# Sliding-window attention on one core: one reciprocal for each query block in place of one for two blocks with lane shuffles

## The chip, the cores and the metric

The kernel runs on one core of one Trainium2 chip. The metric is the device time of one execution in microseconds. The kernel before took 613.11 us in the median of three runs (611.52 to 613.53).

In what follows, TensorE (PE) does the matmuls, VectorE (DVE), ScalarE (ACT) and GpSimd (POOL) the rest of the arithmetic, and SyncE (SP) issues most DMAs. PEld stands for TensorE's weight loads. [...]

## What is computed

Two independent attention problems, A and B, each with its own x, wqkv and wo, in bf16. The outputs stand side by side in the last axis. With S = 2048, D = 1024, 32 heads of 32 columns and a window of 256 keys:

```python
def _A_ref(x, wqkv, wo):
    B, S, D = x.shape
    H = 32; Dh = D // H; W = 256
    qkv = (x @ wqkv).reshape(B, S, 3, H, Dh).transpose(2, 0, 3, 1, 4)
    q, k, v = qkv[0], qkv[1], qkv[2]
    scores = jnp.einsum("bhqd,bhkd->bhqk", q, k) * (Dh ** -0.5)
    idx = jnp.arange(S)
    mask = (idx[:, None] - idx[None, :] >= 0) & (idx[:, None] - idx[None, :] < W)
    scores = jnp.where(mask[None, None], scores, -1e9)
    p = _softmax(scores, axis=-1)
    o = jnp.einsum("bhqk,bhkd->bhqd", p, v)
    return o.transpose(0, 2, 1, 3).reshape(B, S, D) @ wo
```

## The kernel before

**Tiles.** The sequence is cut into 16 blocks of 128. With a window of 256, the queries of block q see the keys of blocks q, q - 1 and q - 2: the first under the diagonal mask, the second whole, the third under the opposite mask. A key block j therefore meets query blocks j, j + 1 and j + 2, and such a pair (j, q) is called an entry. Four heads of 32 columns make a head group g of 128 columns; there are 8 groups in each problem, 16 in all, with 45 entries each.

**Sessions.** Entries are taken in a fixed order, four at a time (SLOTS). One such step is a session, and there are 180. `session` (L438) makes on TensorE the scores of four heads for its four entries into the one tile `st` (L451), ScalarE makes the exponential of all of it into a tile `pt` (L459), and GpSimd sets the masked triangles of the diagonal and of the far entries to zero (L467, L471). GpSimd also does a one-element memset ahead of each DMA that a session starts (L350), which orders the load behind the tile's former users.

**Values and row sums.** `pv` (L486) handles a pair of query blocks p (2p and 2p + 1; 8 pairs in each group, 128 calls) three sessions after the pair's last entry. It takes a bank `acc` (two buffers, so each call needs the one that the call before last used) and accumulates in it, with one 32-column weight tile for each of the four heads, the products of `pt` with V in columns 0 to 255. The row sums of the softmax are matmuls too, with weights of ones. To spare some of them, `edge` (L477) has VectorE add the diagonal entry and the far entry of each query block into the tile `both` (L481) a session earlier, so that a block needs one sum over `both` and one over the middle entry. The call with p = 0 of each group has no far entries and takes no `both`; its sums come straight from `pt`.

The two query blocks of a pair share one area of 128 columns for their row sums: the weights `ones` are two tiles of 32 columns, one with ones in columns 0 to 15 and zeros in the others, one the other way round. So of the 32 lanes of a head, lanes 0 to 15 hold the sums of the first block and lanes 16 to 31 those of the second. VectorE makes one reciprocal of that area into `rinv` (L524). Two lane shuffles (L529) then spread lane 0 or lane 16 over all 32 lanes of a head and so make `wide`, 256 columns. One multiplication (L531) turns `acc` and `wide` into the normalised `oT`, which ends the use of the bank.

**What else TensorE does.** The projections run in chains of eight matmuls or more (L170, in one piece at L172 or in four column pieces at L176): Q and K of a head group, V of two groups, and the output. A chain fills a bank `pp` (two buffers), which ScalarE (L190) or VectorE (L192) then empties with a cast to bf16. After a Q or K chain VectorE also ORs the result's bits into `top` (L184), from which a certificate is made that the fixed shift in the exponential is safe.

**What sets the order.** The kernel is unrolled, and each engine runs its instructions in the order in which the program writes them. For each session the loop at L600 writes: chains that are due (`forced`, L418), the session, the `pv` calls that are due (ahead of which `finish_norm(1)` writes what is left of all but the latest normalisation), the edges due in the next session, and then matmuls of chains up to a budget from `level` (L426). Budgets count the constants NS_MM, NS_ROW and NS_PV and the sizes of the chains.

The planner keeps a model of the time on each engine (`_Clock`, L60). Two things are chosen by it. Which engine empties a bank is the one that would be done first:

```python
best = min(engines, key=lambda e: max(getattr(self, e), self.pe) + COST[e])
```

And small pieces of VectorE's work wait in the list `side` (the ORs, and for each `pv` call the pieces of its normalisation, which go ahead of the ORs). `emit` writes one of them after a matmul step whenever VectorE's modelled time is less than 100 ns ahead of TensorE's or more than eight pieces wait. COST (L37) holds the modelled price of each piece in ns: "rinv" for a reciprocal, "mult" for the shuffles and the multiplication together.

Of the kernel before, what the change touches and what calls it, by code (L numbers as in the profile page):

```python
# [8 lines left out]
BF16 = mybir.dt.bfloat16  # L9
F32 = mybir.dt.float32  # L10
# [3 lines left out]
ALU = mybir.AluOpType  # L14
# [4 lines left out]
P = 128  # L19
# [7 lines left out]
QB = 4  # L27
# [6 lines left out]
PV_LAG = 3  # L34
FREE = 10 ** 6
ACT_EXP = 1800.0
COST = {"act": 590.0, "dve": 670.0, "or": 560.0, "rinv": 930.0, "mult": 900.0,  # L37
        "edge": 620.0}


# [19 lines left out]
class _Clock:  # L60
# [10 lines left out]
    def evacuate(self, engines):  # L71
        best = min(engines, key=lambda e: max(getattr(self, e), self.pe) + COST[e])
        end = max(getattr(self, best), self.pe + 150.0) + COST[best]
        setattr(self, best, end)
# [4 lines left out]
def _fast_path(ctx, tc, cfg, problems, outs, consts, certify):  # L79
    nc = tc.nc  # L80
# [6 lines left out]
    ones = consts["ones"]  # L87
# [23 lines left out]
    vp = ctx.enter_context(tc.tile_pool(name="vt", bufs=2 * NQ))  # L111
    ptp = ctx.enter_context(tc.tile_pool(name="pt", bufs=7))
    edgep = ctx.enter_context(tc.tile_pool(name="edge", bufs=2))
    normp = ctx.enter_context(tc.tile_pool(name="norm", bufs=1))
    osbp = ctx.enter_context(tc.tile_pool(name="osb", bufs=4))
    once = ctx.enter_context(tc.tile_pool(name="once", bufs=1))
    ps_st = ctx.enter_context(tc.tile_pool(name="ps_st", bufs=1, space=PSUM))
    ps_acc = ctx.enter_context(tc.tile_pool(name="ps_acc", bufs=2, space=PSUM))
    ps_proj = ctx.enter_context(tc.tile_pool(name="ps_proj", bufs=2, space=PSUM))

    xT, wqk, wv, wo_sb, vts, oTs, qks, pts = {}, {}, {}, {}, {}, {}, {}, {}
    edges = {}
# [204 lines left out]
    pieces = {}  # L327
# [34 lines left out]
    for m in range(NM):  # L362
        for b in range(0, NB, 512 // (VG * P)):
            k = b // QB
# [5 lines left out]
    for pi in range(NPROB):  # L370
        final = pi == NPROB - 1
        for b in range(NB):
            k = b // QB
# [112 lines left out]
    def pv(g, p):  # L486
        pi, t = divmod(g, T)
        m, u = divmod(g, VG)
        k, h = divmod(p, QB // 2)
        segs = []  # L490
        for j in range(max(2 * p - 2, 0), 2 * p + 2):
            for q in range(max(j, 2 * p), min(j + 3, 2 * p + 2)):
                s, a = place(g, j, q)
                if segs and segs[-1][0] == j and segs[-1][2] == s:
                    segs[-1][4] += 1
                else:
                    segs.append([j, q, s, a, 1])
        acc = ps_acc.tile([P, 512], F32, name="acc")
        clock.pe = max(clock.pe, clock.norms.pop(0))
        moves = [(None, j, (q - 2 * p) * P, n * P, pts[s][:, :, a:a + n, :])  # L500
                 for (j, q, s, a, n) in segs]
        for (j, q, s, a, n) in segs:
            for i in range(n):
                if p == 0 or q + i == j + 1:
                    moves.append((q + i - 2 * p, j, 2 * P, P, pts[s][:, :, a + i:a + i + 1, :]))
        if p:
            both = edges.pop((g, p))
            moves += [(h, 0, 2 * P, P, both[:, :, h:h + 1, :]) for h in range(2)]
        for x, (h, j, o, w_, src) in enumerate(moves):
            for r in range(4):  # L510
                c = u * P + 32 * r
                lhsT = vts[(m, j // QB)][:, j % QB, c:c + 32] if h is None else ones[:, h, :]
                nc.tensor.matmul(acc[32 * r:32 * r + 32, o:o + w_], lhsT=lhsT,  # L513
                                 rhs=src[:, r, :, :], start=(x == 0), stop=(x == len(moves) - 1),
                                 tile_position=(0, 32 * r), skip_group_check=True)
            clock.pe += NS_PV * w_ / P
        if (pi, k) not in oTs:
            oTs[(pi, k)] = opool.tile([P, T, 512], BF16, name="oT")
        rinv = normp.tile([P, P], F32, name="rinv")
        wide = normp.tile([P, 256], F32, name="wide")  # L520
        pieces = []

        def f():
            nc.vector.reciprocal(out=rinv[:], in_=acc[:, 2 * P:3 * P])  # L524
        pieces.append((COST["rinv"], f, False))

        def f():
            for h in range(2):
                nc.vector.stream_shuffle(out=wide[:, h * P:(h + 1) * P], in_=rinv[:],  # L529
                                         mask=[16 * h] * 32)  # L530
            nc.vector.tensor_tensor(out=oTs[(pi, k)][:, t, (p % 2) * 256:(p % 2 + 1) * 256],  # L531
                                    in0=acc[:, 0:256], in1=wide[:], op=ALU.mult)
        pieces.append((COST["mult"], f, True))
        n = max([i + 1 for i, x in enumerate(side) if x[2]], default=0)
        side[n:n] = pieces
# [28 lines left out]
    warm = ps_proj.tile([P, 512], F32, name="pp")  # L564
    for _ in range(5):
        nc.tensor.matmul(warm[:], lhsT=blank[:, 0:P], rhs=blank[:, 0:512], start=True, stop=True)
    flips = [ps_acc.tile([P, 512], F32, name="acc") for _ in range(2)]
    flips = [f[:] for f in flips]
    flips.append(ps_st.tile([P, 4, SLOTS, P], F32, name="st")[:, 0].rearrange("p a q -> p (a q)"))
    flips.append(None)  # L570
    held = [{}, {}]

    def flip(a):
        if a == 3:
            flips[a] = ps_acc.tile([P, 512], F32, name="acc")[:]
        f = flips[a].bitcast(BF16).rearrange("p (ct q) -> p ct q", q=P)
        for ct in range(CT):
            nc.tensor.transpose(out=f[:, ct, :], in_=xrow[a][:, ct * P:(ct + 1) * P],  # L578
                                identity=ident[:])
        dst = xT[(0, 0)][:, :, a * P:(a + 1) * P]  # L580
        half = CT // 2
        nc.scalar.copy(out=dst[:, :half, :], in_=f[:, :half, :])
        nc.vector.tensor_copy(out=dst[:, half:, :], in_=f[:, half:, :])
# [16 lines left out]
    for now in range(END):  # L600
# [3 lines left out]
        while due and due[0][0] <= now:  # L604
            _, pg, pk = due.pop(0)
# [14 lines left out]
    while due:  # L620
        _, pg, pk = due.pop(0)
# [131 lines left out]
@with_exitstack  # L753
def kernel(
    ctx: ExitStack,
    tc: tile.TileContext,
    A_x: bass.AP,
    A_wqkv: bass.AP,
    A_wo: bass.AP,
    B_x: bass.AP,  # L760
    B_wqkv: bass.AP,
    B_wo: bass.AP,
    out: bass.AP,
):
    nc = tc.nc
    S, D = A_x.shape[-2], A_x.shape[-1]
    cfg = _Cfg(S, D)
    problems = [(x.flatten_outer_dims(), wqkv, wo)
                for (x, wqkv, wo) in ((A_x, A_wqkv, A_wo), (B_x, B_wqkv, B_wo))]
    of = out.flatten_outer_dims()  # L770
    outs = [of[:, pi * D:(pi + 1) * D] for pi in range(len(problems))]

    cpool = ctx.enter_context(tc.tile_pool(name="consts", bufs=1))
    ones = cpool.tile([P, 2, 32], BF16, name="ones")
    nc.vector.memset(ones[:], 0.0)
    nc.vector.memset(ones[:, 0, 0:16], 1.0)
    nc.vector.memset(ones[:, 1, 16:32], 1.0)
    ones1 = cpool.tile([P, 1], F32, name="ones1")
    nc.vector.memset(ones1[:], 1.0)
    pm = cpool.tile([P, 1], F32, name="pm")  # L780
    okp = cpool.tile([P, 1], F32, name="okp")
    unsafe_i = cpool.tile([1, 1], I32, name="unsafe_i")
    ident = cpool.tile([P, P], BF16, name="ident")
    nc.gpsimd.memset(ident[:], 0.0)
    nc.gpsimd.affine_select(out=ident[:], in_=ident[:], pattern=[[-1, P]],
                            compare_op=ALU.not_equal, fill=1.0, base=0, channel_multiplier=1)
    consts = {"ones": ones, "ident": ident}
    assert DH * QK_LIMIT * QK_LIMIT * cfg.scale <= CERT

    def reduce_bits(top):  # L790
        seen = top[:]
        nc.vector.tensor_single_scalar(out=seen, in_=seen, scalar=0x7FFF7FFF, op=ALU.bitwise_and)
        nc.vector.tensor_reduce(out=pm[:], in_=seen.bitcast(I16), axis=AX.X, op=ALU.max)
        nc.vector.tensor_scalar(out=okp[:], in0=pm[:], scalar1=float(QK_LIMIT_BITS), scalar2=None,
                                op0=ALU.is_lt)

    def decide(pool):
        csum = pool.tile([P, 512], F32, name="pp")
        nc.tensor.matmul(csum[0:1, 0:1], lhsT=ones1[:], rhs=okp[:], start=True, stop=True)
        nc.vector.tensor_scalar(out=unsafe_i[:], in0=csum[0:1, 0:1], scalar1=float(P) - 0.5,  # L800
                                scalar2=None, op0=ALU.is_lt)

    with tc.manual_schedule():
        with ExitStack() as fctx:
            _fast_path(fctx, tc, cfg, problems, outs, consts, [reduce_bits, decide])

    unsafe = nc.values_load(unsafe_i[0:1, 0:1], min_val=0, max_val=1)

    with tc.If(unsafe > 0, preferred_fallthrough_block=False):
        with ExitStack() as sctx:  # L810
            spool = sctx.enter_context(tc.tile_pool(name="s_consts", bufs=1))
            _make_slow_consts(nc, consts, spool)
            for pi, (x, wqkv, wo) in enumerate(problems):
                with ExitStack() as pctx:
                    _slow_problem(pctx, tc, cfg, x, wqkv, wo, outs[pi], consts)
# [30 lines left out]
```

## Time and profile before

| | |
|---|---|
| median of 3 runs | 613.11 us (611.52 to 613.53) |
| the profiled execution's own time | 613.11 us |
| its span, first to last instruction | 611.4 us |
| granted TensorE clock over the span | 0.999 |
| L524 reciprocal, 128 x 128 | 128 times, 952 ns, 121.9 us |
| L529 shuffle, 128 x 128 | 256 times, 297 ns, 64.4 us of VectorE's time |
| L531 multiplication, 128 x 256 | 128 times, 425 ns, 54.3 us |
| L481 edge addition, 128 x 512 | 224 times, 657 ns, 138.3 us |
| L184 OR, 128 x 256 | 128 times, 505 to 512 ns, 65.1 us |
| casts of `pp` on VectorE (L192) | 60, 675 to 690 ns |
| casts of `pp` on ScalarE (L190), 128 x 512 | 195, 583 to 585 ns |
| exponential (L459), 128 x 2048 | 180 times, 1878 ns |

The page of a profile shows one execution. Its first part gives each engine's busy time, its share of the span and the number of instructions. The chain of work that ended last is followed back from the last instruction, and its shares say which engine the time lay on. The list of waits has who waited for whom, then us in total, how often, and the longest. In a timeline a row has the start in us from the span's beginning, the duration in us, engine, line and operation, the tile written and those read, and in square brackets how long the engine had been idle before and what ended that. Rows of the same kind are merged, with their number behind the x. The ends of matmuls are modelled, so their starts are the surer figure.

The sessions run from about 25 to 570 us. What lies ahead is the first loads and projections; what lies behind is output projections alone.

### The profile page before, as it was taken

How to read it: one execution, taken by the hardware profiler on the slowest of the kernel's cores; microseconds unless marked ns; L12 is line 12 of the kernel's file. 1: busy time of each engine (PE TensorE's matmuls, PEld its weight loads, DVE VectorE, ACT ScalarE, POOL GpSimd, SP SyncE). 2: the span in 40 equal slices, each digit the busy share in tenths (PEclk: the TensorE clock that was granted, in tenths of full speed). 3: DMA queues.
4: the chain of work that ended last, by engine and by line, in shares of the span. 5: the costliest groups of instructions: out<-in, count | busy, mean ns of one | idle time of the engine just before them, and what ended most of it. 6: DMA issues, size and time to landing. Idle time of an engine off the chain costs nothing.

```text
span 611.4 us, 28739 instructions
## 1 busy us (share of the span) xinstructions
PE 594.2 (97%) x12774; PEld 346.0 (57%) x12824; DVE 463.7 (76%) x1193; ACT 445.2 (73%) x382; POOL 328.4 (54%) x630
## 2 busy tenths in 40 slices
PE   7999999999999999999999999999999999999996
PEld 5555466656654655655565765755445664545543
DVE  1477888888799889888888889798897978897200
ACT  3777888888887877867777877777776778776332
POOL 0566566656565666655555656556565556555000
PEclk9999999999999999999999999999999999999999
DMA  9824110111015510444111010112012030114221
GB/s 237 177 71 107 38 38 4 38 38 39 3 26 88 102 37 3 82 96 106 37 29 46 16 27 2 39 36 72 11 44 57 3 106 20 55 48 129 71 78 64
DMA packets 86802, 35.47 MB, mean 58 GB/s; under 512 B 65552, under 2 KB 86160, under 8 KB 86672
## 3 DMA queue, kind: packets, MB, share of 16 engines
q1 hardware_dynamic: 85632, 33.31, 22.6%
q8 instruction: 102, 1.67, 1.2%
q10 hardware_dynamic: 1040, 0.26, 0.2%
q14 instruction: 28, 0.23, 0.1%
HBM read 17.83 MB, written 8.39 MB: 43 GB/s over the span
## 4 chain that ended last, share of the span: by engine, by line
PE 94%; ACT 2%; issue 1%; DMA 1%; DVE 1%; SPq 0%; POOL 0%; ACTq 0%
PE pp L176 43%; PE pp L172 28%; PE acc L513 13%; PE st L451 10%; ACT pt L459 2%; DMA oT<-in_A_x_dram 1%; DVE top L184 0%; DVE both L481 0%; ACT vt L190 0%; PE st L578 0%; ACT kT L190 0%; DVE rinv L524 0%; PE acc L578 0%; SPq L548 0%; POOL pt L467 0%
## 5 line engine op out<-in xcount | busy, mean ns | idle before, releaser
L459 ACT ACTIVATE pt<-st 128x2048 bf16<-128x2048 f32 x180 | 338.0, 1878 | 86.6 <-PE st L451 70.4
L471 POOL TENSOR_SCALAR_AFFINE_SELECT pt<-pt 128x512 bf16<-128x512 bf16 x224 | 155.9, 696 | 145.5 <-ACT pt L459 145.5
L467 POOL TENSOR_SCALAR_AFFINE_SELECT pt<-pt 128x512 bf16<-128x512 bf16 x256 | 179.6, 703 | 87.8 <-ACT pt L459 87.8
L176 PE MATMUL pp<-xT,wqk 128*32 128x512 bf16 x2728 | 164.2, 379 | 1.1 <-POOL wv L350 1.0
L524 DVE RECIPROCAL rinv<-acc 128x128 f32<-128x128 f32 x128 | 121.9, 952 | 56.8 <-PE acc L513 55.6
L481 DVE TENSOR_TENSOR both<-pt 128x512 bf16<-128x512 bf16 x224 | 138.3, 657 | 0.0
L176 PEld LDWEIGHTS <-wqk 128*32 128x32 bf16 x2728 | 70.0, 97 | 55.9 <-DVE both L481 1.1
L172 PE MATMUL pp<-xT,wqk 128*128 128x512 bf16 (+1 forms) x321 | 76.8, 375 | 5.1 <-issue 3.6
L176 PE MATMUL pp<-wv,xT 128*32 128x256 bf16 x2436 | 75.8, 273 | 0.0
L451 PE MATMUL st<-qT,kT 32*128 32x384 bf16 (+2 forms) x1488 | 71.6, 269 | 0.0
L176 PEld LDWEIGHTS <-xT 128*32 128x32 bf16 x2436 | 64.0, 97 | 5.3 <-issue 0.2
L529 DVE STREAM_SHUFFLE wide<-rinv 128x128 f32<-128x128 f32 x256 | 64.4, 297 | 0.0
L513 PE MATMUL acc<-pt,vt 128*32 128x128 bf16 (+1 forms) x2160 | 63.4, 240 | 0.0
L172 PE MATMUL pp<-wo_sb,oT 128*128 128x512 bf16 (+1 forms) x275 | 60.1, 373 | 1.6 <-issue 1.4
L451 PEld LDWEIGHTS <-kT 32*128 32x128 bf16 x1488 | 22.3, 92 | 65.2 <-issue 63.8
L190 ACT CAST osb<-pp 128x512 bf16<-128x512 f32 (+1 forms) x54 | 31.1, 577 | 38.3 <-PE pp L172 25.8
L531 DVE TENSOR_TENSOR oT<-acc,wide 128x256 bf16<-128x256 f32 x128 | 54.3, 425 | 4.4
L172 PEld LDWEIGHTS <-wqk 128*128 128x128 bf16 x358 | 33.6, 100 | 37.1 <-issue 6.9
L176 PE MATMUL pp<-wo_sb,oT 128*32 128x512 bf16 x928 | 54.6, 379 | 0.0
L172 PE MATMUL pp<-wv,xT 128*128 128x256 bf16 x415 | 51.0, 273 | 0.5 <-ACT kT L190 0.2
L513 PEld LDWEIGHTS <-vt 128*32 128x32 bf16 x2160 | 36.0, 96 | 26.3 <-issue 24.0
L172 PEld LDWEIGHTS <-xT 128*128 128x128 bf16 x415 | 38.9, 98 | 11.6 <-issue 5.1
(46 smaller groups left out, 382.3 us busy)
## 6 DMA issues: line engine op xcount, KB each, us to landing
out_dram<-osb SPq DMA_DIRECT2D x63, 128.0 KB, 1.8
wqk<-in_B_wqkv_dram SPq DMA_DIRECT2D x32, 128.0 KB, 2.7
wqk<-in_A_wqkv_dram SPq DMA_DIRECT2D x24, 128.0 KB, 2.9
wo_sb<-in_A_wo_dram SPq DMA_DIRECT2D x16, 128.0 KB, 2.2
wv<-in_B_wqkv_dram SPq DMA_DIRECT2D x16, 128.0 KB, 2.6
wo_sb<-in_B_wo_dram SPq DMA_DIRECT2D x16, 128.0 KB, 2.9
oT<-in_A_x_dram SPq DMA_DIRECT2D x4, 256.0 KB, 5.1
wv<-in_A_wqkv_dram SPq DMA_DIRECT2D x2, 512.0 KB, 6.1
```

The lines of the kernel that those rows point to most:

```text
L172: nc.tensor.matmul(out[:, lo:hi], lhsT=lhsT, rhs=rhs, start=start, stop=stop, skip_group_check=True)
L176: nc.tensor.matmul(out[c:c + 32, lo:hi], lhsT=lhsT[:, c:c + 32], rhs=rhs, start=start, stop=stop, tile_position=(0, c), skip_group_check=True)
L190: nc.scalar.copy(out=out, in_=in_)
L451: nc.tensor.matmul(st[:, r, a:b, :], lhsT=kT[32 * r:32 * r + 32, j * P:(j + 1) * P], rhs=qT[32 * r:32 * r + 32, q * P:(q + b - a) * P], st ...
L459: nc.scalar.activation(out=pt[:, :, :n, :].rearrange("p r a q -> p r (a q)"), in_=st[:, :, :n, :].rearrange("p r a q -> p r (a q)"), func= ...
L467: nc.gpsimd.affine_select(out=blk, in_=blk, pattern=[[0, 4], [1, P]], compare_op=ALU.is_ge, fill=0.0, base=0, channel_multiplier=-1)
L471: nc.gpsimd.affine_select(out=blk, in_=blk, pattern=[[0, 4], [-1, P]], compare_op=ALU.is_gt, fill=0.0, base=0, channel_multiplier=1)
L481: nc.vector.tensor_tensor(out=both[:, :, h, :], in0=pts[s0][:, :, a0, :], in1=pts[s1][:, :, a1, :], op=ALU.add)
L513: nc.tensor.matmul(acc[32 * r:32 * r + 32, o:o + w_], lhsT=lhsT, rhs=src[:, r, :, :], start=(x == 0), stop=(x == len(moves) - 1), tile_pos ...
L524: nc.vector.reciprocal(out=rinv[:], in_=acc[:, 2 * P:3 * P])
L529: nc.vector.stream_shuffle(out=wide[:, h * P:(h + 1) * P], in_=rinv[:], mask=[16 * h] * 32)
L531: nc.vector.tensor_tensor(out=oTs[(pi, k)][:, t, (p % 2) * 256:(p % 2 + 1) * 256], in0=acc[:, 0:256], in1=wide[:], op=ALU.mult)
```

## The change

Each query block gets its own 128 columns of row sums. The bank `acc` is now two halves of 256 columns: half 0 the values, half 1 the row sums of both blocks side by side, in all 32 lanes of a head. The weights are one tile of 32 columns of ones. The sums over `both` of the two blocks are one group of matmuls of 256 columns in place of two of 128. VectorE makes two reciprocals of 128 columns, each a piece of its own, straight into a tile `rinv` of 256 columns, and the multiplication follows as the third piece; the shuffles and the tile `wide` go. The price "mult" becomes 430 ns from 900, so that a normalisation is counted as 930 + 930 + 430 in place of 930 + 900. `rinv` has two buffers in place of one. Nothing in the loads, the sessions or the projections is edited.

```diff
-COST = {"act": 590.0, "dve": 670.0, "or": 560.0, "rinv": 930.0, "mult": 900.0,
+COST = {"act": 590.0, "dve": 670.0, "or": 560.0, "rinv": 930.0, "mult": 430.0,
...
-    normp = ctx.enter_context(tc.tile_pool(name="norm", bufs=1))
+    misc = ctx.enter_context(tc.tile_pool(name="misc", bufs=2))
...
-        acc = ps_acc.tile([P, 512], F32, name="acc")
+        acc = ps_acc.tile([P, 2, 256], F32, name="acc")
...
-        moves = [(None, j, (q - 2 * p) * P, n * P, pts[s][:, :, a:a + n, :])
+        moves = [(0, j, (q - 2 * p) * P, n * P, pts[s][:, :, a:a + n, :])
...
-                    moves.append((q + i - 2 * p, j, 2 * P, P, pts[s][:, :, a + i:a + i + 1, :]))
+                    moves.append((1, j, (q + i - 2 * p) * P, P, pts[s][:, :, a + i:a + i + 1, :]))
         if p:
-            both = edges.pop((g, p))
-            moves += [(h, 0, 2 * P, P, both[:, :, h:h + 1, :]) for h in range(2)]
-        for x, (h, j, o, w_, src) in enumerate(moves):
+            moves.append((1, 0, 0, 2 * P, edges.pop((g, p))))
+        for x, (which, j, o, w_, src) in enumerate(moves):
             for r in range(4):
                 c = u * P + 32 * r
-                lhsT = vts[(m, j // QB)][:, j % QB, c:c + 32] if h is None else ones[:, h, :]
-                nc.tensor.matmul(acc[32 * r:32 * r + 32, o:o + w_], lhsT=lhsT,
+                lhsT = ones[:, 0:32] if which else vts[(m, j // QB)][:, j % QB, c:c + 32]
+                nc.tensor.matmul(acc[32 * r:32 * r + 32, which, o:o + w_], lhsT=lhsT,
...
-        rinv = normp.tile([P, P], F32, name="rinv")
-        wide = normp.tile([P, 256], F32, name="wide")
+        rinv = misc.tile([P, 256], F32, name="rinv")
         pieces = []
+        for a in range(2):
+            def f(a=a):
+                nc.vector.reciprocal(out=rinv[:, a * P:(a + 1) * P],
+                                     in_=acc[:, 1, a * P:(a + 1) * P])
+            pieces.append((COST["rinv"], f, False))
 
         def f():
-            nc.vector.reciprocal(out=rinv[:], in_=acc[:, 2 * P:3 * P])
-        pieces.append((COST["rinv"], f, False))
-
-        def f():
-            for h in range(2):
-                nc.vector.stream_shuffle(out=wide[:, h * P:(h + 1) * P], in_=rinv[:],
-                                         mask=[16 * h] * 32)
-            nc.vector.tensor_tensor(out=oTs[(pi, k)][:, t, (p % 2) * 256:(p % 2 + 1) * 256],
-                                    in0=acc[:, 0:256], in1=wide[:], op=ALU.mult)
+            nc.vector.tensor_tensor(out=oTs[(pi, k)][:, t, h * 256:(h + 1) * 256],
+                                    in0=acc[:, 0, :], in1=rinv[:], op=ALU.mult)
         pieces.append((COST["mult"], f, True))
...
-    ones = cpool.tile([P, 2, 32], BF16, name="ones")
-    nc.vector.memset(ones[:], 0.0)
-    nc.vector.memset(ones[:, 0, 0:16], 1.0)
-    nc.vector.memset(ones[:, 1, 16:32], 1.0)
+    ones = cpool.tile([P, 32], BF16, name="ones")
+    nc.vector.memset(ones[:], 1.0)
```

The tiles of the first transposes (`flips`) take the new shape of `acc` and are viewed flat; that changes nothing else. In the multiplication h is p % 2, as before.

More of the change, by code (lines that the diff above doesn't have):

```diff
@@ L566, in _fast_path @@
         nc.tensor.matmul(warm[:], lhsT=blank[:, 0:P], rhs=blank[:, 0:512], start=True, stop=True)
-    flips = [ps_acc.tile([P, 512], F32, name="acc") for _ in range(2)]
-    flips = [f[:] for f in flips]
+    flips = [ps_acc.tile([P, 2, 256], F32, name="acc") for _ in range(2)]
+    flips = [f[:].rearrange("p a q -> p (a q)") for f in flips]
     flips.append(ps_st.tile([P, 4, SLOTS, P], F32, name="st")[:, 0].rearrange("p a q -> p (a q)"))
@@ L574, in flip @@
         if a == 3:
-            flips[a] = ps_acc.tile([P, 512], F32, name="acc")[:]
+            flips[a] = ps_acc.tile([P, 2, 256], F32, name="acc")[:].rearrange("p a q -> p (a q)")
         f = flips[a].bitcast(BF16).rearrange("p (ct q) -> p ct q", q=P)
```

## The prediction

> **What bounds the kernel now.** I read the engines' busy shares first, then the chain that ended last, then the waits, then VectorE's rows in the timeline. TensorE is over 90% busy in 38 of the 40 slices, and the chain lies on it:
>
> ```profile
> PE 594.2 (97%) x12774; PEld 346.0 (57%) x12824; DVE 463.7 (76%) x1193; ACT 445.2 (73%) x382; POOL 328.4 (54%) x630
> ...
> PE 94%; ACT 2%; issue 1%; DMA 1%; DVE 1%; SPq 0%; POOL 0%; ACTq 0%
> ```
>
> A busy share of modelled matmul ends could hide gaps, so I took start-to-start distances of TensorE's rows. In the session stage (25 to 570 us) a 512-column matmul follows the last by 215 ns, a 256-column one by 110, a 128-column one by 55, hardly ever more. The places where TensorE really stands still are few: five banks not yet emptied by ScalarE (at 77, 138, 187, 199 and 232 us, 2.0 us beyond the usual distance) and one stop at 262.7 us, about 1.2, which begins after a row of seven DMA_TRANSPOSE issues and has no VectorE work behind it. So an instruction of VectorE matters only through a buffer that TensorE needs back: the two `acc` banks (emptied by L531), the two `pp` banks (L192 or, on ScalarE, L190), and the `both` tiles of L481 that it reads. The waits say how much room VectorE has:
>
> ```profile
> DVE rinv L524 <- PE acc L513: 55.6, 61, 3.3
> ...
> PEld L513 <- DVE oT L531: 0.6, 3, 0.2
> ```
>
> In 61 of the 128 normalisations VectorE had stood idle for the row sums, 55.6 us in all. TensorE's wait for L531 is 0.6 us in the whole run. The stage's row has VectorE at 456.35 of 545 us (84%), ScalarE at 421.5 (77%).
>
> **What the change does to TensorE.** Its program keeps its order: `emit`, `level` and `forced` count NS_ constants and chain sizes, and COST enters only `evacuate` and `run_side`, that is, which of two engines empties a bank and where VectorE's pieces stand. Transposed loads, POOL's order and SP's order stay too; the diff moves no load. Inside `pv` the 120 blocks with p > 0 lose one of two 128-column groups over `both` and have one of 256 columns: 2 x 55 becomes 110 ns. The rows show where that would be seen:
>
> ```profile
> 300.29 0.28 PE L513 MATMUL acc<-pt,ones 128*32 128x128 bf16 x8
> 300.40 0.28 PE L513 MATMUL acc<-both,ones 128*32 128x128 bf16 x8
> 300.52 0.39 PE L176 MATMUL pp<-wo_sb,oT 128*32 128x512 bf16 x4
> ```
>
> Two groups took 300.40 to 300.52, no gap between. Saving: 120 x 0 to 3 ns, at most 0.4 us; I take **-0.2**. Two memsets fewer at the start: TensorE's first useful transposes wait for the DMA of x (4.08, 6.00, 7.80 us), which covers them: 0.
>
> **What it does to VectorE.** One normalisation now:
>
> ```profile
> 375.60 0.96 DVE L524 RECIPROCAL rinv<-acc 128x128 f32<-128x128 f32 x1 [0.30 <-PE acc L513]
> 376.60 0.01 DVE L529 LOAD_MASK_SELECT wide<-rinv  x1
> 376.60 0.30 DVE L529 STREAM_SHUFFLE wide<-rinv 128x128 f32<-128x128 f32 x1
> 376.81 0.01 DVE L529 LOAD_MASK_SELECT wide<-rinv  x1
> 376.81 0.29 DVE L529 STREAM_SHUFFLE wide<-rinv 128x128 f32<-128x128 f32 x1
> 377.14 0.42 DVE L531 TENSOR_TENSOR oT<-acc,wide 128x256 bf16<-128x256 f32 x1
> 377.48 0.41 DVE L184 TENSOR_TENSOR top<-top,kT 128x256 int32<-128x256 int32 x1
> 377.81 1.62 DVE L481 TENSOR_TENSOR both<-pt 128x512 bf16<-128x512 bf16 x2
> 379.36 0.68 DVE L192 CAST vt<-pp 128x512 bf16<-128x512 f32 x1
> ```
>
> From the reciprocal's start to the multiplication's end: 375.60 to 377.56, 1.96 us (111 normalisations that nothing interrupts have 1.94 to 1.97). The two shuffles with their mask loads cost 0.54 of it (376.60 to 377.14). They go; a second reciprocal of the same shape, 0.956, comes. Independent neighbours here start 0.08 before the last one ends (379.36 + 0.68 against the L184 row at 379.96), dependent ones 0.04 after. So the block becomes 0.956 + 0.956 - 0.08 + 0.04 + 0.425 = 2.30 us: **+0.34 each**, 128 x 0.34 = 43.5 us more VectorE work; +0.42 (54 us) if the second reciprocal doesn't overlap the first. In the stage VectorE goes from 84% to (456 + 43.5) / 545 = 92%. The shared engine is not full, so it is no new bound by sum; what counts is whether a later row reaches a bank too late.
>
> [...]
>
> **From VectorE's delay to TensorE's waits.** I walked down VectorE's rows in order of time: add 0.34 at each L531, and before every row take off the idle time that stood there (91 us in all, 0.30 of it at 375.60 above). What is left is that row's delay. At the multiplications it is 0.34 (0.44 in the middle, 0.74 for the ninth in ten, 1.36 at most). Then each user's spare time, TensorE's start less the end of the work that it needs:
>
> - `acc`: from L531's end to the pair's next-but-one `pv` block. Three places have 0.95 us, the rest over 2.4. No delay reaches it. 0 us.
> - `both`: from L481's end to its first matmul: 1.20 at least, median 2.34. One place ties. 0 us.
> - `pp` emptied by VectorE, 60 times: median spare 1.06 us, but a tenth of them have 0.3 or less. Seven of the 60 come late if each stays where it is. The case in the fence: this cast ends at 380.03 and the matmuls of the next chain but one start on that bank at 380.08. The delay there is 0.43 left from before 375.60 plus 0.34, no idle time after it: 0.77, so 0.72 too late. The seven (near 169, 370, 379, 436, 445, 454 us, and one tie) add up to **+2.6 us**.
>
> The planner, though, is told of the price (COST of a normalisation 1830 to 2290) and may give those casts to ScalarE. I bound that by the same rows: with all 60 on ScalarE behind whatever it runs then (an exponential lasts 1.88, a cast 0.58), the late ones add up to 4.5 us; with the better engine at each of the 60, to 1.7. With +0.42 instead of 0.34 and no change of engine it is 6.0, and 0.9 more from `both` and `acc`. I take 2.6, since it rests on the rows as they stand; 1.7 and 6.9 are kept as ends, and 0 if the planner finds places that none of these rows show. The exponential is not in danger: the next session's scores start 0.35 to 0.85 us after the last exponential's end in nine of ten sessions, and in all 179 at the same 0.10 us after TensorE's preceding work, so they wait for TensorE and not for it.
>
> The last normalisation ends at 571.2 us and some 35 us of output matmuls follow, so 0.34 there costs nothing.
>
> **Sum.** The profiled execution took 613.11 us (span 611.4, 1.7 outside it), which is also the median of the three. 613.1 - 0.2 + 2.6 = **615.5 us**.
>
> **Rivals.** A measurement of this kernel can tell about 0.3% (1.8 us) from no change.
>
> 1. *Covered.* The 55.6 us of idle time before reciprocals and the moved casts absorb all. For it: only seven places of 60 are late, and the planner's price for a normalisation, 1830 before against 1960 in the rows, becomes right (2290 against 2300). Against: those places have 0.05 to 0.56 us of spare, and ScalarE's own stalls are what TensorE waits for now. 613.1 - 0.2 + 0 to 0.9: 612.9 to 613.8.
> 2. *Faster.* Place: the five `pp` stalls behind ScalarE. If the truer price moves those casts, too, to a free engine, up to 2.0 us goes: 613.1 - 0.2 - 2.0 = 610.9. It decides if VectorE is free within some 0.5 us of the end of those five chains; against it, VectorE is the busier engine and gets 10% more.
> 3. *VectorE becomes the bound.* Where four `pv` blocks follow at one session each (p = 6, 7, 0, 1, at 15 seams between head groups), four normalisations of 2.30 and edges of 1.1 to 1.6 us per block meet sessions of 2.9 to 3.1 us. The window from 225 to 275 us already has 43.61 of 50 busy; 12 x 0.34 makes it 47.7, 95%. If the backlog isn't worked off there, `acc` comes late by some 0.4 to 0.5 us at each seam: +6 to +7, 619.5. For it: the three `acc` places with 0.95 us of spare show that backlogs happen; against: elsewhere the spare is 2.4 and more.
>
> **Chances.** Forecast (614.0 to 617.5) 0.58, of which 0.10 lies under 614.9; covered 0.21; faster by over 0.3% 0.06; bound by VectorE 0.15. So faster 0.06, within 0.3% 0.31, slower 0.63. The range reaches from the covered case to the third rival: 612.5 to 619.8.
>
> **What would show it.** Right: 256 reciprocals of about 0.95 us, no shuffle, VectorE's total near 505 us; the idle time before reciprocals well under 55.6; a few more places where a first matmul on `pp` waits for L190 or L192, 2 to 4 us more in all; fewer than 60 casts on VectorE; TensorE's busy time unchanged. Wrong: waits of L513 for the multiplication in the tens (rival 3), the five stalls gone (rival 2), a second reciprocal that costs much more or less than 0.87 start to start, or selects on POOL that change their 0.70.

## The result and the profile after

The changed kernel takes 617.78 us (median of 4 runs, 616.84 to 618.02), the kernel before 612.82 us beside it (4 runs). The ratio is 1.0081, with a 95% interval of 1.0060 to 1.0101: slower by 5.0 us, where 2.4 were forecast. The profiled execution took 617.96 us with a span of 616.2.

The page of the changed kernel, first the busy times, then the shares of the chain:

```profile
PE 596.2 (97%) x12326; PEld 345.6 (56%) x12376; DVE 474.8 (77%) x772; ACT 461.6 (75%) x417; POOL 320.9 (52%) x630
...
PE 89%; ACT 6%; issue 2%; DMA 1%; SPq 0%; DVE 0%; POOL 0%; DVEq 0%; ACTq 0%
```

VectorE grew by 11 us only, though it got 128 more reciprocals. ScalarE grew by 16 and went from 2% of the chain to 6%; VectorE fell from 1% to 0. The reason stands in the casts: 25 of 257 are on VectorE now, 60 were. The planner, told of the higher price, gave 38 to ScalarE and 3 the other way. So the late engine is not the one that got the work. All 16 late casts of the table below stand directly behind an exponential; five of them were late before, and the other eleven stood on VectorE. The timeline of the changed kernel at one such place, PE, ACT and DVE rows alone:

```profile
370.22 1.88 ACT L459 ACTIVATE pt<-st 128x2048 bf16<-128x2048 f32 x1 [0.75 <-PE st L451]
...
370.32 1.89 PE L172 MATMUL pp<-xT,wqk 128*128 128x512 bf16 x8 [0.16 <-issue]
370.48 1.18 DVE L481 TENSOR_TENSOR both<-pt 128x512 bf16<-128x512 bf16 x2
371.59 0.41 DVE L184 TENSOR_TENSOR top<-top,qT 128x256 int32<-128x256 int32 x1
371.99 0.58 ACT L190 CAST qT<-pp 128x512 bf16<-128x512 f32 x1
...
372.62 0.81 PE L172 MATMUL pp<-xT,wqk 128*128 128x512 bf16 x3 [0.41 <-ACT qT L190]
```

The cast of `qT` stands behind an exponential of 1.88 us and starts at 371.99; TensorE needs its bank (a `pp` buffer of 128 x 512 fp32) at 372.05 and gets it at 372.62, 0.57 us late. VectorE had ended its edge additions near 371.6 and then did an OR that nobody waited for. In the kernel before this cast stood on VectorE (369.86 there) and cost at most 0.18:

```profile
368.69 2.71 PE L172 MATMUL pp<-xT,wqk 128*128 128x512 bf16 x11 [0.16 <-issue]
...
369.86 0.68 DVE L192 CAST qT<-pp 128x512 bf16<-128x512 f32 x1
```

I went through all TensorE starts that come later than the usual distance and sorted them by what ended just before. Between the profiled executions (+4.8 us of span):

| | before | changed |
|---|---|---|
| stalls behind ScalarE's casts, 25 to 560 us | 5, 2.0 us | 16, 5.9 us |
| stalls behind VectorE's casts, 25 to 560 us | 3, 0.5 us | 0 |
| stop near 263 us, the start of problem B | 1.5 us | 1.0 us |
| stop near 565 us, the certificate | 0 | 1.2 us |
| first session's start | 16.27 | 16.85 |
| end of the span after the last matmul's start | 5.70 | 6.08 |

The first, second and fourth line make +4.6. The third, fifth and sixth vary from execution to execution, as the experiments show (the sixth between 5.6 and 6.3). The lines sum to 5.1, 0.3 more than the spans differ by; in those 0.3 lie the forecast -0.2 for TensorE and what I can't put down to a place.

The stop near 565 us is a second effect that the prediction did not have. The changed kernel, rows of PE and DVE:

```profile
561.78 0.42 DVE L184 TENSOR_TENSOR top<-top,kT 128x256 int32<-128x256 int32 x1
562.24 0.29 DVE L786 TENSOR_SCALAR top<-top 128x256 int32<-128x256 int32 x1
562.57 0.69 DVE L787 TENSOR_REDUCE pm<-top 128x1 f32<-128x512 int16 x1
563.29 0.15 DVE L788 TENSOR_SCALAR okp<-pm 128x1 f32<-128x1 f32 x1
563.37 1.46 DVE L481 TENSOR_TENSOR both<-pt 128x512 bf16<-128x512 bf16 x2
...
564.75 0.94 DVE L522 RECIPROCAL rinv<-acc 128x128 f32<-128x128 f32 x1
564.88 0.29 PE L512 MATMUL acc<-both,ones 128*32 128x256 bf16 x4 [0.23 <-DVE both L481]
...
565.62 0.08 DVE L794 TENSOR_SCALAR unsafe_i<-pp 1x1 int32<-1x1 f32 x1
...
565.77 3.64 PE L176 MATMUL pp<-wo_sb,oT 128*32 128x512 bf16 x64 [0.60 <-DVE unsafe_i L794]
```

Seven ORs since 558.10 (the last of them at 561.78) and the certificate's reduction stand in VectorE's queue ahead of the edge additions that `pv` needs: TensorE waits 0.43 us for `both`. Then the decision (L794) stands behind a reciprocal, and holds a `pp` bank for 0.78 us.

### The profile page after: what moved, and what is told of

Same layout as the page of the kernel before. It is cut to its first block, busy times and chain, and to the rows that moved or that the text cites. A ratio compares the mean times of both kernels' runs of the same rounds, so it can differ in the third digit from the quotient of the medians.

```text
span 616.2 us, 27471 instructions
## 1 busy us (share of the span) xinstructions
PE 596.2 (97%) x12326; PEld 345.6 (56%) x12376; DVE 474.8 (77%) x772; ACT 461.6 (75%) x417; POOL 320.9 (52%) x630
## 4 chain that ended last, share of the span: by engine, by line
PE 89%; ACT 6%; issue 2%; DMA 1%; SPq 0%; DVE 0%; POOL 0%; DVEq 0%; ACTq 0%
PE pp L176 42%; PE pp L172 25%; PE acc L512 13%; PE st L451 10%; ACT pt L459 4%; DMA oT<-in_A_x_dram 1%; ACT kT L190 1%; ACT vt L190 1%; DMA xT<-in_B_x_dram 0%; ACT qT L190 0%; PE st L574 0%; ACT osb L190 0%; PE acc L574 0%; SPq L544 0%; DVE rinv L522 0%
## 5 line engine op out<-in xcount | busy, mean ns | idle before, releaser
L522 DVE RECIPROCAL rinv<-acc 128x128 f32<-128x128 f32 x256 | 226.3, 924 | 62.7 <-PE acc L512 62.0
L471 POOL TENSOR_SCALAR_AFFINE_SELECT pt<-pt 128x512 bf16<-128x512 bf16 x224 | 152.9, 683 | 153.1 <-ACT pt L459 150.3
L467 POOL TENSOR_SCALAR_AFFINE_SELECT pt<-pt 128x512 bf16<-128x512 bf16 x256 | 175.6, 688 | 90.7 <-ACT pt L459 90.7
L481 DVE TENSOR_TENSOR both<-pt 128x512 bf16<-128x512 bf16 x224 | 126.8, 608 | 0.0
L176 PEld LDWEIGHTS <-wqk 128*32 128x32 bf16 x2728 | 73.0, 97 | 57.3 <-issue 2.9
L190 ACT CAST osb<-pp 128x512 bf16<-128x512 f32 (+1 forms) x57 | 32.9, 577 | 38.1 <-PE pp L172 24.3
L527 DVE TENSOR_TENSOR oT<-acc,rinv 128x256 bf16<-128x256 f32 x128 | 54.3, 424 | 4.1
L172 PEld LDWEIGHTS <-oT 128*128 128x128 bf16 x288 | 27.3, 98 | 32.4 <-issue 2.4
```

Source lines behind the costliest of these rows:

```text
L172: nc.tensor.matmul(out[:, lo:hi], lhsT=lhsT, rhs=rhs, start=start, stop=stop, skip_group_check=True)
L176: nc.tensor.matmul(out[c:c + 32, lo:hi], lhsT=lhsT[:, c:c + 32], rhs=rhs, start=start, stop=stop, tile_position=(0, c), skip_group_check=True)
L190: nc.scalar.copy(out=out, in_=in_)
L467: nc.gpsimd.affine_select(out=blk, in_=blk, pattern=[[0, 4], [1, P]], compare_op=ALU.is_ge, fill=0.0, base=0, channel_multiplier=-1)
L471: nc.gpsimd.affine_select(out=blk, in_=blk, pattern=[[0, 4], [-1, P]], compare_op=ALU.is_gt, fill=0.0, base=0, channel_multiplier=1)
L481: nc.vector.tensor_tensor(out=both[:, :, h, :], in0=pts[s0][:, :, a0, :], in1=pts[s1][:, :, a1, :], op=ALU.add)
```

## Experiments: the planner's choice or VectorE's work

Theory A after this reading: the loss is the planner's choice, casts moved behind exponentials, and not the time that the second reciprocal takes. Theory B, the prediction's sum: VectorE's added work makes things late. The change does both at once, so the first two kernels do one each. All runs are compared with the kernel before on the same chip, in five rounds.

**The plan alone.** The kernel before, its own instructions, in three pieces at the new prices, so that the planner decides as in the changed kernel:

```diff
-COST = {... "rinv": 930.0, "mult": 900.0,
+COST = {... "rinv": 930.0, "mult": 430.0,
...
                 nc.vector.stream_shuffle(out=wide[:, h * P:(h + 1) * P], in_=rinv[:],
                                          mask=[16 * h] * 32)
+        pieces.append((COST["rinv"], f, False))
+
+        def f():
             nc.vector.tensor_tensor(...)
```

> The kernel before with its own instructions (one reciprocal, two shuffles, one multiplication), but planned with the new price: three pieces at 930, 930 and 430. Theory A, the planner's choice costs the time (38 casts fewer on VectorE, and ScalarE's casts come late behind exponentials): 25 casts on VectorE, some 16 stalls of TensorE behind ScalarE with 5.9 us in all (2.0 before), 3 to 4 us over the kernel before, 616 to 617. Theory B, VectorE's added work costs the time: no more than 0.5 us over before, 613.

617.97 us, ratio 1.0074 (1.0059 to 1.0090). That is the whole loss, with no work added, and a microsecond more than expected. Its page and the same place in its timeline:

```profile
PE 595.9 (97%) x12774; PEld 346.1 (56%) x12824; DVE 436.6 (71%) x1158; ACT 461.6 (75%) x417; POOL 327.1 (53%) x630
```
```profile
372.18 0.41 DVE L184 TENSOR_TENSOR top<-top,qT 128x256 int32<-128x256 int32 x1
...
372.68 0.58 ACT L190 CAST qT<-pp 128x512 bf16<-128x512 f32 x1
...
373.31 0.81 PE L172 MATMUL pp<-xT,wqk 128*128 128x512 bf16 x3 [0.41 <-ACT qT L190]
```

VectorE is at 71%, less busy than in either kernel, and the execution is as slow as the changed one. 25 casts on VectorE, 16 stalls behind ScalarE, 5.9 us: place by place those of the changed kernel, and the stop near 565 us is there too (1.2 us).

**The work alone.** The changed kernel's instructions in two pieces at the old prices, 930 for both reciprocals and 900 for the multiplication:

```diff
-COST = {... "mult": 430.0,
+COST = {... "mult": 900.0,
...
-        for a in range(2):
-            def f(a=a):
+        def f():
+            for a in range(2):
                 nc.vector.reciprocal(...)
-            pieces.append((COST["rinv"], f, False))
+        pieces.append((COST["rinv"], f, False))
```

> The changed kernel's instructions, planned with the old price: two pieces at 930 (both reciprocals) and 900, so that every cast stays on the engine that it had before. The walk down VectorE's rows in the prediction: 60 casts on VectorE, seven of them late by 2.6 us in all, 615.5. Theory A alone, with the choice as the whole cause: 613. Theory B: the whole loss, 617 to 618.

614.39 us, ratio 1.0029 (1.0016 to 1.0041): 1.0 to 2.5 us. 60 casts on VectorE, 5 stalls behind ScalarE as before (2.0 us), 7 behind VectorE with 2.3 us in all (3 with 0.5 before), none near 565 us. This is the case that the prediction worked out with 2.6 us; it lost 1.5 us by the medians, and 1.9 us by the stalls behind VectorE in its trace. One of them, in its timeline:

```profile
310.38 1.77 DVE L523 RECIPROCAL rinv<-acc 128x128 f32<-128x128 f32 x2 [0.78 <-PE acc L512]
...
312.07 0.63 DVE L192 CAST vt<-pp 128x512 bf16<-128x512 f32 x1
...
312.75 0.40 PE L176 MATMUL pp<-xT,wqk 128*32 128x512 bf16 x4 [0.47 <-DVE vt L192]
```

The cast stands behind two reciprocals, and TensorE is 0.65 us late at that bank. So the work has a price of its own where casts remain behind it; but it is the smaller one, and the two don't add up: in the changed kernel the casts have left VectorE, and its 0.27 us per block meet nobody.

**Less work on VectorE, same plan.** The changed kernel without the 128 ORs, whose pieces still stand in the planner's list:

```diff
         def f():
-            nc.vector.tensor_tensor(out=top[:], in0=top[:], in1=dst.bitcast(I32),
-                                    op=ALU.bitwise_or)
+            pass
```

> The changed kernel and its plan, with the 128 ORs of the certificate left out (so that part of the safety check isn't computed): VectorE has 65 us less to do, and every other instruction stays on its engine and in its place. Theory A: the stalls behind ScalarE's casts stay (some 16, 5.9 us) and only the stop near 565 us goes: 616 to 616.7. Theory B, VectorE is too full: the loss goes, 613.

616.22 us, ratio 1.0050 (1.0034 to 1.0066). VectorE is down to 407.6 us, 66%, and the 16 stalls behind ScalarE stand at the same places with the same 5.9 us; the one at 372.62 is now

```profile
371.29 0.58 ACT L189 CAST qT<-pp 128x512 bf16<-128x512 f32 x1
...
371.92 0.59 PE L172 MATMUL pp<-xT,wqk 128*128 128x512 bf16 x2 [0.41 <-ACT qT L189]
```

0.57 us late as before. Only the stop near 565 us went. Theory B falls for the changed kernel: freeing VectorE of more than the change put on it does not give the time back.

**The certificate later.** The changed kernel with reduction and decision among the last output projections:

```diff
-        if now >= sealed and len(certify) == 2:
-            while side:
-                run_side()
-            certify.pop(0)(top)
-        elif now >= sealed + 2 and len(certify) == 1:
-            certify.pop(0)(ps_proj)
...
     finish_norm()
+    while side:
+        run_side()
+    certify.pop(0)(top)
+    emit(END + 10, 6 * NS_MM * CT)
+    certify.pop(0)(ps_proj)
     emit(END + 10, float("inf"))
```

> The changed kernel with the certificate's reduction and decision moved from sessions 176 and 178 to the stage of output projections alone. If the 1.2 us that TensorE stood still near 565 us (0.43 for the edge tile, 0.78 for the bank that the decision reads) is VectorE's queue behind the ORs and the reduction: 1.2 us under the changed kernel, 616.6, and both waits gone. If the late normalisations cause it: they stand still there as before, 617.8.

616.51 us, ratio 1.0059 (1.0044 to 1.0075). In its trace neither wait near 565 us is left, and a new one of 0.4 us stands at the decision (586 us). The time agrees with what was expected, but its interval overlaps the changed kernel's, so it is the trace that shows this part.

## Experiments: how far the price reaches

If the price decides, it should work both ways on the kernel before, with no other edit than this one; and the true price should be the best if the planner's model is right.

```diff
-COST = {... "mult": 900.0,
+COST = {... "mult": 1030.0,
```

Two more kernels have 650.0 and 430.0 there.

> The kernel before with the price of shuffles and multiplication at 1030 in place of 900, so that a normalisation is counted as the 1960 ns that it takes. If a dearer VectorE alone moves casts behind exponentials, whether the price is true or not: between 60 and 25 casts on VectorE, more stalls behind ScalarE than before's five, 613.5 to 616. If the true price is the best one: 612 to 613, stalls not more than before.

> The kernel before with only the price of shuffles and multiplication lowered from 900 to 650, so that the planner gives more casts to VectorE. If the planner's price sets the loss through stalls behind ScalarE's casts: fewer than the five stalls of before (2.0 us), some late casts on VectorE in their place, 611.5 to 613. If any other engine choice than that of before is only worse, as chance would have it: 613.5 to 616.

> The kernel before with that price at 430, so that a normalisation is counted as 1360 where it takes 1960. If the price has an optimum above the true one and VectorE's queue has the room that its idle time suggests: 611 to 613, no stall behind ScalarE's casts left. If VectorE's casts now stand behind its own work: stalls behind VectorE of 3 us or more, 615 to 617.

The kernel before, by the price of a whole normalisation (it takes 1960 ns):

| counted as | casts on VectorE | stalls behind ScalarE | behind VectorE | ratio (95%) |
|---|---|---|---|---|
| 1360 | 84 | 1, 0.5 us | 2, 0.5 us | 0.9983 (0.9970 to 0.9997) |
| 1580 | 77 | 1, 0.6 us | 3, 0.8 us | 0.9983 (0.9971 to 0.9996) |
| 1830 (before) | 60 | 5, 2.0 us | 3, 0.5 us | 1 |
| 1960 (true) | 45 | 10, 3.6 us | 1, 0.2 us | 1.0020 (1.0008 to 1.0031) |
| 2290 (x1, in three pieces) | 25 | 16, 5.9 us | 0 | 1.0074 (1.0059 to 1.0090) |

Stalls under 0.11 us are left out of the table. The true price is worse than the one that was too low by 130 ns. At 1360 VectorE does more than in any other of these, and the kernel has the lowest median, 611.32 us against 613.02 beside it:

```profile
PE 593.3 (97%) x12774; PEld 345.3 (57%) x12824; DVE 482.5 (79%) x1217; ACT 434.3 (71%) x358; POOL 325.6 (53%) x630
```

It beats both kernels, the one before by about 0.17%, of which the interval leaves 0.03 to 0.30. From 1580 it can't be told apart.

The same on the changed kernel's instructions, with the two pieces at 930 and 430:

> The changed kernel's instructions (two reciprocals) with a normalisation counted as 930 + 430 where it takes 2300. If what the changed kernel lost came from the price and not from the added reciprocal: near the 614.4 of the same instructions at the old price, 613 to 615.5. If VectorE's added 43 us come through as soon as it gets more casts: 616 to 619, stalls behind VectorE.

614.04 us, ratio 1.0021 (1.0008 to 1.0033), with 84 casts on VectorE, one stall over 0.11 us behind ScalarE (0.5 us) and nine behind VectorE (3.7). So of the 5.0 us that the change lost, about 3.7 come back by the plan, with the instructions unchanged, and 0.5 to 2.0 us stay against the kernel before at its own price. That is not the whole price of the second reciprocal, since the kernel before gains by the lower price too: at the same 1360 and on the same chip it took 611.32, 2.7 us less, where the work alone had cost 1.5 at 1830.

**ScalarE made dearer.** The changed kernel with the exponential counted as 2300 ns:

```diff
-ACT_EXP = 1800.0
+ACT_EXP = 2300.0
```

> The changed kernel with its own prices for VectorE, but the exponential counted as 2300 ns in place of 1800 (it takes 1878), so that ScalarE looks busier and casts go back to VectorE. If the casts behind exponentials are the loss: more casts on VectorE than 25, fewer stalls behind ScalarE than 16, 614 to 616.5. If not: 617.8.

617.73 us, ratio 1.0074 (1.0060 to 1.0089): a miss. 45 casts are on VectorE, 20 more, but 14 stalls behind ScalarE with 5.4 us remain: the casts that moved were mostly not the late ones. And two new kinds of wait came, 1.1 us for a multiplication at 43 us and 0.8 us near 565. So the number of casts on VectorE is not itself the cause; which casts, is. Why the planner's clocks put just those fourteen on ScalarE, I have not settled.

**One reciprocal of 256 columns.** The work-alone kernel with both reciprocals in one instruction:

```diff
-            for a in range(2):
-                nc.vector.reciprocal(out=rinv[:, a * P:(a + 1) * P],
-                                     in_=acc[:, 1, a * P:(a + 1) * P])
+            nc.vector.reciprocal(out=rinv[:], in_=acc[:, 1, :])
```

> The changed kernel's instructions at the old price, but the two reciprocals of 128 columns made one instruction of 256. If a reciprocal costs by the element: about 1.85 us for it, the block 2.31, and the time that of two reciprocals at the old price, 614.4. If half of the 952 ns is paid per instruction: 1.4 us, the block 1.87 and so shorter than before's 1.96, 612.5 to 613.

614.06 us, ratio 1.0023 (1.0012 to 1.0034), the same as two. The row, from its timeline:

```profile
375.03 1.76 DVE L522 RECIPROCAL rinv<-acc 128x256 f32<-128x256 f32 x1 [0.29 <-PE acc L512]
```

## Why the prediction was right in direction and half in size

- *TensorE's program*: right. No late start remains that isn't a wait for a bank, a tile or a load; the -0.2 us is too small to be seen in the sum.
- *The block on VectorE*: 2.30 us forecast; two reciprocals start 0.874 us apart and the second takes 0.895 (medians of the changed kernel), so it is 0.874 + 0.895 + 0.04 + 0.425 = 2.23, which is also the median measured there, and the growth 0.27 in place of 0.34. The sum had priced the second reciprocal like the first, 0.956.
- *The walk down VectorE's rows*: its total came near, its places mostly not, so the agreement is in part luck. With the engines kept, seven places were forecast with 2.6 us, and seven stalls came, 1.9 us more than before. Those near 169, 370 and 379 us were named, but they were late before already (0.15, 0.18 and 0.13 us) and grew by only 0.1 each. The 0.05 us that the walk took for spare time at 380 is the distance at which a waiting matmul follows its cast (0.050 to 0.055 in every stall counted here), and the 0.43 that it took as left over from before was not there: in the work-alone kernel that reciprocal still stands idle for 0.29 us, and the cast behind it starts 3.86 us after it where it was 3.76. The three largest, 0.44 at 293, 0.65 at 313 and 0.43 at 401 us, were not named. There the cast stands between the reciprocals and the multiplication, and has the whole second reciprocal, 0.87, ahead of it; the walk added 0.34, and only at the multiplication.
- *The term that failed*: "I take 2.6, since it rests on the rows as they stand". It rested on casts that would stay on VectorE, and the same paragraph said that the planner may move them. They moved; the bound worked out for that case, 4.5 us with all 60 on ScalarE, was the nearer one (3.9 us more with 38 moved). With it the sum would have been 617.4; that the measured 617.78 lies so close is chance in part, since the stalls on `pp` came to 3.4 more (3.9 behind ScalarE, 0.5 fewer behind VectorE) and the next point was in no sum. I had the price edit in the diff, and a planner that compares finishing times, and should have taken the end at which its comparison points.
- *Left out*: the certificate, 1.2 us. The walk had ORs in VectorE's rows but did not ask where the planner puts them when it thinks VectorE is busier: into a heap that is written just ahead of the last edge additions.
- *Rivals*: "covered" was right that no cast on VectorE would be late (none over 0.11 us is), but not about the moved ones. "Faster" had the sign of the planner's effect wrong, because it took a truer price for a better plan; the price series shows the reverse. "VectorE becomes the bound" is refuted: at 66%, 71% and 77% of VectorE the stalls behind ScalarE are the same.
- *What would show it*: fewer than 60 casts on VectorE and 2 to 4 us more stalls on `pp` came true; idle time before reciprocals "well under 55.6" did not (62.0 us), since VectorE got rid of casts, and for the same reason its total did not come near 505 us (474.8). A sign of being wrong was selects on POOL that change their 0.70 us: their mean went to 0.685, and to 0.654 without the ORs, but no stall counted here ends with one.

## What to carry to other kernels

Where a program is laid out by a planner, an edit of a cost is a change by itself: run it alone, with the old instructions, before putting the loss down to the new ones. A shared engine that is "too busy" in the model can be idle in the trace (VectorE is at 71% with the plan alone); look for where TensorE stood still and ask which queue the late instruction stood in, and only then who has more work. A price in such a planner is a weight to be tuned on the chip: here the true one lost to one 600 ns too low.

## What the runs showed of the hardware

A reciprocal on VectorE cost by the column in the two lengths measured: for 128 columns of fp32 out of `acc` 956 ns alone (kernel before), 957 as the first and 895 as the second of a pair (changed kernel; all three are medians), for 256 in one instruction 1.76 us (the row of the run with one reciprocal). From 957 to 1760 that is an estimated 6.3 ns a column and some 0.15 us besides. A pair takes 0.874 + 0.895 = 1.77 us, so splitting cost 0.01 us.

The first session starts at 16.27 us in the kernel before and at 16.85 in the changed one. The matmuls up to there are the same, but TensorE comes to its closer spacing at different times. The first matmuls on x, kernel before and changed:

```profile
11.19 3.40 PE L172 MATMUL pp<-xT,wqk 128*128 128x256 bf16 x24
```
```profile
11.10 4.07 PE L172 MATMUL pp<-xT,wqk 128*128 128x256 bf16 x24
```

In both, 256-column matmuls follow each other by 213 ns at first and by 109 later; the turn is at 12.46 us in the one and at 13.7 in the other. That is 0.6 us of the 4.8 between the two spans, and not the change. The stop near 263 us, at the first loads of problem B, was 1.5 us long in the one and 1.0 in the other. A difference of a microsecond between two executions of this kernel has to be looked for at these two places first.
